# Top-k attention and a SwiGLU block on one core: weight rounding in pieces of 512 columns, the first K and Q split over two queues by head, and the first rounding step moved behind the start of the first top-k

## The chip, the core and the metric

The kernel runs on one core of one Trainium2 chip. The metric is the device time in microseconds (us) of one execution, lower being better; where several runs are taken, their median counts. Five units work side by side, each on its own list of instructions in order: TensorE (PE, matrix products; PEld is its weight load), VectorE (DVE), ScalarE (ACT), GpSimd (POOL) and the queues that issue DMA transfers (SP, and a few on ACT).[...]

## The reference

Attention keeps, for each query, the 32 largest of its 576 scores; the result goes through a gated feed-forward block (FFN). All is in 32-bit floats.

```python
# q, k, v: (8, 8, 576, 64)          top_k = 32
scores = scale * np.matmul(q, k.transpose(0, 1, 3, 2))
kth    = np.partition(scores, -top_k, axis=-1)[..., -top_k:-top_k + 1]
scores = np.where(scores >= kth, scores, -1000000000.0)
attn   = softmax(scores)                        # over the last axis
x      = (attn @ v).transpose(0, 2, 1, 3).reshape(4608, 512)
g      = x @ w_gate                             # (4608, 1536)
out    = (g * sigmoid(g) * (x @ w_val)) @ w_out # (4608, 512)
```

The weights arrive as 64-bit floats. The kernel reads them as pairs of 32-bit integers and makes 32-bit floats of them itself ("rounding" below).

## The kernel before

**Attention in units.** A unit is one batch, one tile of 128 queries and one pair of heads; there are 8 x 5 x 4 = 160 of them, and every fifth tile of a batch has only 64 queries, so that its two heads share the 128 partitions and the unit has half the work. For each unit PE makes the scores (L306 or L292), ACT copies them to SBUF (L311, L297), and DVE finds the 32 largest by four rounds of MAX8 (L327) with a MATCH_REPLACE8 (L331) between rounds, then writes a penalty for the values below the 32nd (L337). POOL adds the penalty to the scores (L349), ACT takes the exponential (L358) and scales it by the reciprocal of the sum (L370 on DVE, L373 on ACT), PE transposes the weights (`etps`, L385) and multiplies by V (L405, L414), and ACT copies the result into `xT` (L429).

**FFN in blocks.** The 4608 tokens form 18 blocks of 256. As soon as all four head pairs of a block are done, `feed` makes its products with `w_gate` and `w_val` (L468), the gate on ACT and POOL (L493 to L501), and the product with `w_out`. It gives these out in pieces of some 1.7 us of PE time. Block 0 uses a plain product (L514); the later ones use a scheme with seven instead of eight quarter products (L554), whose sums and differences of `w_out` POOL makes beforehand (L168 to L185).

**The order is written out by hand.** One loop over the units (L705 on) interleaves everything: unit n's top-k on DVE, the scores of unit n+1, the exponential of n-1, the transposes of n-3, the product with V of n-4, and FFN pieces paid from a credit (4.45 pieces for a full unit in the first 28 units, later a share that follows the unit's own PE work). At the end, a dependency without semaphore pins that order on PE, DVE, ACT and POOL. DMA issues on SP are not pinned.

**Weight rounding.** `rounded` handles one piece of 128 x 256 values in five stages: load 256 KB (L109); on ACT the absolute value of the high words and a scaling of the low words (L114, L116); on POOL a clamp (L119); on DVE a shift and mask (L123), followed on POOL by an integer addition (L126); on DVE a merge with sign and exponent into the destination `wg`, `wv` or `wo` (L129). There are 24 pieces for each of the three weights, 72 in all. `weights` is a generator; each of its steps moves several pieces by one stage, `lags` (L153) steps apart: at step n, piece n is loaded, piece n-2 has its ACT and clamp stages, piece n-3 its shift and addition, piece n-5 its merge. `early` (L158, called at L738) brings the ACT stage of the newest pieces forward at the start of a unit. Six buffers of each kind are in turn (`bufs=6`). A step is taken by `rounding(1)`, called in `dve` (L713 to L720): every VALUES step of the top-k adds 5/11 to `due`, and one step of rounding is due at each whole number, except in the first four steps of a unit (`beside=False`). Two steps are taken before the loads of the second pair of heads (L693), two more between the first unit's scores and the loop (L697). `need` makes more steps where an FFN product asks for a piece that isn't there yet; it takes the number of pieces.

**The first loads.** `load(i)` brings K and Q of a pair of heads: for each of K and Q one DMA per head, then one for the last 64 positions of both heads. For the first pair, K goes over SP and Q over ACT's queue (L217); all other loads go over SP.

Of the kernel before, what the change touches and what calls it, by code (L numbers as in the profile page):

```python
# [10 lines left out]
FP32 = mybir.dt.float32  # L11
I32 = mybir.dt.int32
# [3 lines left out]
P = 128  # L16
# [5 lines left out]
WP = 256  # L22
# [5 lines left out]
def kernel(  # L28
# [37 lines left out]
    nc = tc.nc  # L66
    B, H, S, D = q.shape
    DM, DFF = w_gate.shape
# [4 lines left out]
    KC = DM // P  # L73
    MC = DFF // P
    MS = MC // 2
    MQ = MC // 2
# [9 lines left out]
    conv = ctx.enter_context(tc.tile_pool(name="conv", bufs=2))  # L86
    ffn = ctx.enter_context(tc.tile_pool(name="ffn", bufs=2))
# [13 lines left out]
    wg = consts.tile([P, KC, DFF], FP32, name="wg")  # L101
    wv = consts.tile([P, KC, DFF], FP32, name="wv")
    wo = consts.tile([P, MC, DM], FP32, name="wo")

    def rounded(src, dst):

        n = dst.shape[1]
        w = ffn.tile([P, n, 2], I32, tag="w", name="w", bufs=6)
        nc.sync.dma_start(w[:], src.bitcast(I32).rearrange("p (f t) -> p f t", t=2))  # L109
        yield  # L110
        low, high = w[:, :, 0], w[:, :, 1]

        size = conv.tile([P, n], FP32, tag="size", name="size", bufs=6)
        nc.scalar.activation(size[:], high.bitcast(FP32), AF.Abs)  # L114

        nc.scalar.mul(low, low.bitcast(U32), 2.0**-29)  # L116
        yield

        nc.gpsimd.tensor_scalar(size[:], size[:], HUGE, LEAST, ALU.min, ALU.max)  # L119
        yield  # L120

        bits = size[:].bitcast(I32)
        nc.vector.tensor_scalar(  # L123
            bits, bits, 3, 0x3FFFFFFF, ALU.logical_shift_left, ALU.bitwise_and
        )
        nc.gpsimd.tensor_tensor(bits, bits, low, ALU.add)  # L126
        yield

        nc.vector.scalar_tensor_tensor(  # L129
            out=dst.bitcast(I32), in0=high, scalar=-0x40000000, in1=bits,  # L130
            op0=ALU.bitwise_and, op1=ALU.bitwise_or,
        )

    def weights():

        pieces = []
        for f in range(0, DFF, WP):
            for src, dst in ((w_gate, wg), (w_val, wv)):
                for c in range(KC):
                    pieces.append((src[c * P : (c + 1) * P, f : f + WP], dst[:, c, f : f + WP]))  # L140
        for c in range(MC):
            for f in range(0, DM, WP):
                pieces.append((w_out[c * P : (c + 1) * P, f : f + WP], wo[:, c, f : f + WP]))
        pieces = [rounded(*p) for p in pieces]
        step = [0] * len(pieces)

        def upto(i, k):

            while 0 <= i < len(pieces) and step[i] < k:
                next(pieces[i], None)  # L150
                step[i] += 1

        lags = (5, 3, 2, 2, 0)  # L153
        for n in range(len(pieces) + lags[0]):
            for k, lag in enumerate(lags):
                upto(n - lag, len(lags) - k)
            ready[0] = max(n - lags[0] + 1, 0)
            early[0] = lambda: [upto(n - 1, 2), upto(n, 2)]  # L158
            yield
        early[0] = lambda: None  # L160


        add, sub = ALU.add, ALU.subtract
        lo, hi = slice(0, DM // 2), slice(DM // 2, DM)
        for m in range(0, MQ, 2):
            mm, nn = slice(m, m + 2), slice(MQ + m, MQ + m + 2)
            t3 = ffn.tile([P, 2, DM // 2], FP32, tag="w", name="t3", bufs=6)
            nc.gpsimd.tensor_tensor(t3[:], wo[:, nn, hi], wo[:, mm, hi], sub)  # L168
            T[7] += [t3[:, i, :] for i in range(2)]
            yield  # L170
        while not plain_done:
            yield
        for m in range(0, MQ, 2):
            mm, nn = slice(m, m + 2), slice(MQ + m, MQ + m + 2)
            t1 = wo[:, mm, hi]
            nc.gpsimd.tensor_tensor(t1, t1, wo[:, mm, lo], sub)
            T[5] += [wo[:, m + i, hi] for i in range(2)]
            yield
            t2 = ffn.tile([P, 2, DM // 2], FP32, tag="w", name="t2", bufs=6)
            nc.gpsimd.tensor_tensor(t2[:], wo[:, nn, hi], t1, sub)  # L180
            T[6] += [t2[:, i, :] for i in range(2)]
            yield
            for i in range(2):
                t4 = conv.tile([P, DM // 2], FP32, tag="size", name="t4", bufs=6)
                nc.gpsimd.tensor_tensor(t4[:], wo[:, MQ + m + i, lo], t2[:, i, :], sub)  # L185
                T[4].append(t4[:])
            yield
        T[1] += [wo[:, m, lo] for m in range(MQ)]
        T[2] += [wo[:, MQ + m, lo] for m in range(MQ)]
        T[3] += [wo[:, MQ + m, hi] for m in range(MQ)]  # L190
        yield

    ready = [0]
    early = [lambda: None]
    plain_done = []
    T = {i: [] for i in range(1, 8)}
    weight = weights()

    def rounding(n):
        for _ in range(n):  # L200
            next(weight, None)

    def need(n):

        while ready[0] < n:
            next(weight)
# [4 lines left out]
    def load(i):  # L211
        b, hp = pairs[i]
        h = slice(2 * hp, 2 * hp + 2)
        kq = ld.tile([P, 2, J, 2, D], FP32, tag="kq", name="kq_in")
        kq_last = ld.tile([P, 2, D], FP32, tag="kql", name="kq_last")
        for n, src in ((0, k), (1, q)):
            queue = nc.scalar if n == 1 and i == 0 else nc.sync  # L217
            for hh in range(2):
                queue.dma_start(
                    kq[:, n, :, hh, :],  # L220
                    src[b, 2 * hp + hh, 0:JP].rearrange("(p j) d -> p j d", j=J),
                )
            queue.dma_start(
                kq_last[n * R : (n + 1) * R], src[b, h, JP:S].rearrange("h p d -> p h d")
            )
        raw[i] = (kq, kq_last)
# [209 lines left out]
    def store(o, g0):  # L436

        at = g0
        while at < g0 + P:
            b, c = divmod(at, S)  # L440
            j, p0 = divmod(c, P)
            n = min(g0 + P - at, S - c, P - p0)
            r0 = b * S + (c if j == J else J * p0 + j)
            dst = out[r0 : r0 + n, :] if j == J else out[r0 : r0 + J * (n - 1) + 1 : J, :]
            nc.sync.dma_start(dst, o[at - g0 : at - g0 + n, :])
            at += n
# [3 lines left out]
    def flush(queue):  # L450
        while queue:
            queue.pop(0)()

    def feed(kb):
# [6 lines left out]

        def product(w, s, then):
            ps = ps_f.tile([P, 2, BLK], FP32, tag="f", name="f")
            need(8 * s + (4 if w is wg else 8))
            for i in range(2):
                m = 2 * s + i
                for kc in range(KC):
                    nc.tensor.matmul(  # L468
                        ps[:, i, :],
                        w[:, kc, m * P : (m + 1) * P],  # L470
                        x[:, kc, :],
                        start=(kc == 0),
                        stop=(kc == KC - 1),
                    )
                if i == 1:
                    on_act.append(lambda: then(ps))
                yield 1
# [28 lines left out]
        if plain:  # L506
            for t in range(2):
                ps = ps_f.tile([P, DM], FP32, tag="f", name="o_ps")
                for m in range(MC):
                    need(8 * MS + 2 * m + 2)  # L510
                    if m == 6:
                        flush(on_act)
                        flush(on_pool)
                    nc.tensor.matmul(  # L514
                        ps[:],
                        hs[m // 2][:, m % 2, t * P : (t + 1) * P],
                        wo[:, m, :],
                        start=(m == 0),
                        stop=(m == MC - 1),
                    )  # L520
                    if m == MC - 1:

                        def finish(ps=ps, t=t):
                            nc.scalar.copy(o[:, t, :], ps[:])
                            store(o[:, t, :], kb * BLK + t * P)

                        on_act.append(finish)
                        if t == 1:
                            plain_done.append(True)
                    if m % 2 == 1:  # L530
                        yield 1
            return
# [149 lines left out]
    def run(steps):  # L682
        for _ in steps:
            pass
# [7 lines left out]
    load(0)  # L692
    rounding(2)  # L693
    load(1)
    run(fetch(0))
    run(scores(0))
    rounding(2)  # L697
    run(fetch(1))
    credit = [0.0]
    no = iter(())  # L700
    over = {}
    TURN, VALUES = 3, 4
    HEAD = 28
    due = [0.0]
    for n in range(NU + VALUES):  # L705
        nh = n_heads(units[n][1]) if n < NU else 1
        topk = select(n) if n < NU else no
# [106 lines left out]
```

## Time and profile before

Median of three runs: 1845.41 us (1844.97 to 1846.03). The profiled execution has a span of 1843.6 us.

| engine | busy us | share of span |
|---|---|---|
| PE | 1708.1 | 93% |
| DVE | 1623.5 | 88% |
| ACT | 1208.6 | 66% |
| POOL | 1026.2 | 56% |

| the rounding's instructions, 128x256 | engine | count | busy us | mean ns |
|---|---|---|---|---|
| L114 absolute value | ACT | 72 | 31.9 | 443 |
| L116 scaling | ACT | 72 | 31.6 | 439 |
| L119 clamp | POOL | 72 | 32.0 | 444 |
| L123 shift and mask | DVE | 72 | 21.3 | 296 |
| L126 addition | POOL | 72 | 54.4 | 755 |
| L129 merge into `wg`, `wv` | DVE | 48 | 19.4 | 404 |
| L129 merge into `wo` | DVE | 24 | 15.2 | 631 |

Shares of busy time are averages over stages that differ: in the first stage there are no FFN blocks to feed, and PE has little to do; in the last, DVE has finished. Mean durations on DVE include the overlap of an instruction's start with the end of the one before it, so the distance from start to start is what an instruction costs. The weights are rounded in the first 236 us. FFN work starts at 158 us.

### The profile page before, as it was taken

What the parts mean: (1) busy time and instruction counts of PE and PEld (TensorE: products, weight loads), DVE (VectorE), ACT (ScalarE), POOL (GpSimd) and SP (SyncE); (2) the same over time, 40 slices, a digit from 0 to 9 for tenths busy, and PEclk for the clock granted to TensorE, in tenths of its full rate; (3) what the DMA queues carried; (4) which work ended last, traced back from release to release, by engine and by line L of the source; (5) the groups of instructions that cost most, each with busy time, mean ns of one, the idle gap of its engine ahead of it and who ended that gap; (6) DMA issues with size and microseconds to landing.
All of it is one profiled execution on the core that took longest, in us unless ns stands there. A gap on an engine that the chain in (4) does not pass through costs nothing.

```text
span 1843.6 us, 30858 instructions
## 1 busy us (share of the span) xinstructions
PE 1708.1 (93%) x10756; PEld 1409.2 (76%) x10756; DVE 1623.5 (88%) x3477; ACT 1208.6 (66%) x3015; POOL 1026.2 (56%) x1007
## 2 busy tenths in 40 slices
PE   3447899999999989999999999999999999999998
PEld 2336658777788878887888878888788878888887
DVE  7999999999999979997999989998999989998400
ACT  5667757667666667676767675767676776675432
POOL 4666756645455644656464736564556554646444
PEclk7668999989999999999999999999999999999999
DMA  7332221000300021000300012000300011000000
GB/s 191 92 86 81 69 53 40 12 1 8 86 1 13 1 59 34 13 1 14 73 19 1 13 36 57 2 12 2 73 19 12 1 36 32 1 12 12 1 12 12
DMA packets 111260, 59.67 MB, mean 32 GB/s; under 512 B 89088, under 2 KB 97280, under 8 KB 111104
## 3 DMA queue, kind: packets, MB, share of 16 engines
q1 hardware_dynamic: 109904, 57.41, 11.8%
q8 instruction: 85, 1.39, 0.3%
q14 instruction: 71, 0.58, 0.1%
q10 hardware_dynamic: 1200, 0.30, 0.1%
HBM read 48.23 MB, written 9.44 MB: 31 GB/s over the span
## 4 chain that ended last, share of the span: by engine, by line
PE 83%; DVE 6%; ACT 3%; POOL 3%; issue 2%; DMA 0%; POOLq 0%; ACTq 0%
PE f L468 39%; PE x_ps L554 9%; PE av L414 8%; PE etps L385 7%; PE s L306 7%; PE y_ps L554 6%; DVE m L327 2%; DVE rest L331 2%; PE s L292 2%; PE av L405 1%; PE o_ps L514 1%; PE kqps L261 1%; POOL e L349 1%; ACT e L358 1%; DVE e L337 1%
## 5 line engine op out<-in xcount | busy, mean ns | idle before, releaser
L327 DVE MAX8 m<-rest 128x8 f32<-128x576 f32 x864 | 614.5, 745 | 2.2
L331 DVE MATCH_REPLACE8 rest<-m,rest 128x576 f32<-128x576 f32 x576 | 423.4, 741 | 0.0
L349 POOL TENSOR_TENSOR e<-e,sc 128x1152 f32<-128x1152 f32 (+1 forms) x160 | 382.7, 2392 | 67.2 <-DVE e L337 61.7
L468 PE MATMUL f<-xT,wg 128*128 128x256 f32 x1728 | 401.7, 382 | 0.0
L468 PE MATMUL f<-xT,wv 128*128 128x256 f32 x1728 | 398.9, 381 | 0.0
L468 PEld LDWEIGHTS f<-xT,wg 128*128 128x128 f32 x1728 | 322.8, 190 | 62.5 <-issue 20.5
L468 PEld LDWEIGHTS f<-xT,wv 128*128 128x128 f32 x1728 | 324.5, 190 | 58.5 <-issue 16.3
L496 POOL TENSOR_TENSOR h<-h,half_g 128x512 f32<-128x512 f32 x108 | 138.2, 1279 | 295.2 <-ACT h L495 289.6
L327 DVE MAX8 m<-sc 128x8 f32<-128x576 f32 x288 | 205.1, 748 | 99.1 <-ACT sc L297 58.3
L385 PE MATMUL etps<-ident,e 128*128 128x128 f32 (+1 forms) x1312 | 186.7, 287 | 104.3 <-POOL size L126 36.2
L358 ACT ACTIVATE e<-e,bias 128x576 f32<-128x576 f32 x288 | 222.1, 777 | 93.3 <-POOL e L349 93.2
L386 ACT COPY et<-etps 128x512 f32<-128x512 f32 (+1 forms) x448 | 184.3, 483 | 124.3 <-PE etps L385 122.9
L385 PEld LDWEIGHTS etps<-ident,e 128*128 128x128 f32 (+1 forms) x1312 | 159.6, 147 | 133.1 <-POOL size L126 39.0
L501 POOL TENSOR_TENSOR h<-h,val 128x512 f32<-128x512 f32 x108 | 140.2, 1298 | 193.2 <-ACT val L500 193.1
L373 ACT ACTIVATE e<-e,tot 128x576 f32<-128x576 f32 x288 | 211.9, 789 | 6.3 <-DVE tot L370 6.3
L331 DVE MATCH_REPLACE8 rest<-m,sc 128x576 f32<-128x576 f32 x288 | 211.6, 740 | 0.0
L306 PE MATMUL s<-kqT 64*128 64x288 f32 x1024 | 171.1, 447 | 4.4 <-ACT kqT L266 3.8
L414 PE MATMUL av<-et,v 128*64 128x128 f32 (+1 forms) x2560 | 173.8, 281 | 0.0
L337 DVE TENSOR_SCALAR e<-sc,m 128x576 f32<-128x576 f32 x288 | 165.4, 610 | 3.4
L311 ACT COPY sc<-s 128x288 f32<-128x288 f32 x512 | 163.9, 402 | 1.9 <-PE s L306 1.9
L414 PEld LDWEIGHTS av<-et,v 128*64 128x64 f32 x2560 | 136.8, 144 | 23.0 <-issue 7.1
L493 ACT ACTIVATE h<-f 128x512 f32<-128x512 f32 x108 | 65.4, 605 | 132.6 <-PE f L468 132.6
(71 smaller groups left out, 2042.1 us busy)
## 6 DMA issues: line engine op xcount, KB each, us to landing
kq_in<-in_k_dram SPq DMA_DIRECT2D x64, 128.0 KB, 2.8
v<-in_v_dram SPq DMA_DIRECT2D x32, 256.0 KB, 2.9
kq_in<-in_q_dram SPq DMA_DIRECT2D x62, 128.0 KB, 2.9
w<-in_moe_w_gate_dram SPq DMA_DIRECT2D x24, 256.0 KB, 2.7
w<-in_moe_w_val_dram SPq DMA_DIRECT2D x24, 256.0 KB, 2.7
w<-in_moe_w_out_dram SPq DMA_DIRECT2D x24, 256.0 KB, 2.5
out_dram<-o SPq DMA_DIRECT2D x40, 128.0 KB, 2.4
out_dram<-o SPq DMA_DIRECT2D x16, 256.0 KB, 2.4
```

The source lines that it names most:

```text
L306: nc.tensor.matmul(ps[:, 0:half], slab[d, q0 : q0 + P], slab[d, k0 : k0 + half])
L327: nc.vector.max(m[:, t, 8 * r : 8 * r + 8], cur[:, hs])
L331: nc.vector.match_replace(rest[:, hs], m[:, t, 8 * r : 8 * r + 8], cur[:, hs], LOWEST)
L337: nc.vector.tensor_scalar(e[:, hs], sc[:, hs], m[:, t, TOP_K - 1 : TOP_K], FAR, ALU.is_lt, ALU.mult)
L349: nc.gpsimd.tensor_tensor(e[:, every], e[:, every], sc[:, every], ALU.add)
L358: nc.scalar.activation(e[:, hs], e[:, hs], AF.Exp, bias=bias[:, t : t + 1], scale=scale, accum_out=tot[:, t : t + 1],)
L373: nc.scalar.mul(e[:, hs], e[:, hs], tot[:, t : t + 1])
L385: nc.tensor.transpose(ps[0:kl, c * P : (c + 1) * P], e[:, k0 : k0 + kl], ident[:])
L386: nc.scalar.copy(et[0:kl, c0 : c0 + cn, :], ps[0:kl, 0 : cn * P].rearrange("p (c j) -> p c j", c=cn),)
L414: nc.tensor.matmul(av[hh * R : (hh + 1) * R, 0:ql], v_last[:, hh, :] if c == J else vt[:, hh, c, :], moving, start=last and c == 0, stop=c ...
L468: nc.tensor.matmul(ps[:, i, :], w[:, kc, m * P : (m + 1) * P], x[:, kc, :], start=(kc == 0), stop=(kc == KC - 1),)
L554: nc.tensor.matmul(ps, lhsT, T[i][m], start=m == 0, stop=m == MQ - 1)
```

## The change

It does three things.

1. A piece is now 128 x 512 values: two row blocks of `w_gate` or `w_val`, or a whole row block of `w_out`. There are 36 pieces instead of 72, with three buffers of twice the size. A step of the generator now moves a piece only where `n - lag` is even, so that a piece takes the same number of steps as two pieces did. `need` counts in the new pieces. The temporary tiles of POOL's sums and differences of `w_out` are cut from three tiles allocated at once, and the last difference of each group is one instruction of 512 columns instead of two of 256.
2. Of the first pair's K and Q, head 0 goes over SP and head 1 over ACT's queue; the small loads of the last positions all go over SP.
3. The two steps of rounding ahead of the loop go away; `due` starts at 2 instead, so that they are taken behind the first two MAX8 of the first unit.

Its purpose is to spend fewer instructions, each with its fixed cost, on the rounding, and to let the first top-k start earlier.

```diff
     def rounded(src, dst):
-        n = dst.shape[1]
-        w = ffn.tile([P, n, 2], I32, tag="w", name="w", bufs=6)
-        nc.sync.dma_start(w[:], src.bitcast(I32).rearrange("p (f t) -> p f t", t=2))
+        w = ffn.tile([P, 2, WP, 2], I32, tag="w", name="w", bufs=3)
+        nc.sync.dma_start(w[:].rearrange("p c f t -> p c (f t)"), src.bitcast(I32))
         yield
-        low, high = w[:, :, 0], w[:, :, 1]
-        size = conv.tile([P, n], FP32, tag="size", name="size", bufs=6)
+        low, high = w[:, :, :, 0], w[:, :, :, 1]
+        size = conv.tile([P, 2, WP], FP32, tag="size", name="size", bufs=3)
...
         lags = (5, 3, 2, 2, 0)
-        for n in range(len(pieces) + lags[0]):
+        for n in range(2 * len(pieces) - 1 + lags[0]):
             for k, lag in enumerate(lags):
-                upto(n - lag, len(lags) - k)
-            ready[0] = max(n - lags[0] + 1, 0)
-            early[0] = lambda: [upto(n - 1, 2), upto(n, 2)]
+                if (n - lag) % 2 == 0:
+                    upto((n - lag) // 2, len(lags) - k)
+            ready[0] = max((n - lags[0]) // 2 + 1, 0)
+            early[0] = lambda: upto(n // 2, 2)
             yield
...
-            for i in range(2):
-                t4 = conv.tile([P, DM // 2], FP32, tag="size", name="t4", bufs=6)
-                nc.gpsimd.tensor_tensor(t4[:], wo[:, MQ + m + i, lo], t2[:, i, :], sub)
+            t4 = conv.tile([P, 2, DM // 2], FP32, tag="size", name="t4", bufs=3)
+            nc.gpsimd.tensor_tensor(t4[:], wo[:, nn, lo], t2, sub)
...
         for n, src in ((0, k), (1, q)):
-            queue = nc.scalar if n == 1 and i == 0 else nc.sync
             for hh in range(2):
+                queue = nc.scalar if hh == 1 and i == 0 else nc.sync
                 queue.dma_start(kq[:, n, :, hh, :], ...)
-            queue.dma_start(kq_last[n * R : (n + 1) * R], ...)
+            nc.sync.dma_start(kq_last[n * R : (n + 1) * R], ...)
...
     run(scores(0))
-    rounding(2)
     run(fetch(1))
...
-    due = [0.0]
+    due = [2.0]
```

More of the change, by code (lines that the diff above doesn't have):

```diff
@@ L105, in rounded @@
     def rounded(src, dst):
-        n = dst.shape[1]
-        w = ffn.tile([P, n, 2], I32, tag="w", name="w", bufs=6)
-        nc.sync.dma_start(w[:], src.bitcast(I32).rearrange("p (f t) -> p f t", t=2))
+        w = ffn.tile([P, 2, WP, 2], I32, tag="w", name="w", bufs=3)
+        nc.sync.dma_start(
+            w[:].rearrange("p c f t -> p c (f t)"), src.bitcast(I32)
+        )
         yield
-        low, high = w[:, :, 0], w[:, :, 1]
-        size = conv.tile([P, n], FP32, tag="size", name="size", bufs=6)
+        low, high = w[:, :, :, 0], w[:, :, :, 1]
+        size = conv.tile([P, 2, WP], FP32, tag="size", name="size", bufs=3)
         nc.scalar.activation(size[:], high.bitcast(FP32), AF.Abs)
@@ L138, in weights @@
             for src, dst in ((w_gate, wg), (w_val, wv)):
-                for c in range(KC):
-                    pieces.append((src[c * P : (c + 1) * P, f : f + WP], dst[:, c, f : f + WP]))
+                for c in range(0, KC, 2):
+                    rows = src[c * P : (c + 2) * P, f : f + WP]
+                    pieces.append((
+                        rows.rearrange("(c p) f -> p c f", p=P), dst[:, c : c + 2, f : f + WP]
+                    ))
         for c in range(MC):
-            for f in range(0, DM, WP):
-                pieces.append((w_out[c * P : (c + 1) * P, f : f + WP], wo[:, c, f : f + WP]))
+            pieces.append((
+                w_out[c * P : (c + 1) * P].rearrange("p (c f) -> p c f", c=2),
+                wo[:, c].rearrange("p (c f) -> p c f", c=2),
+            ))
         pieces = [rounded(*p) for p in pieces]
@@ L164, in weights @@
         lo, hi = slice(0, DM // 2), slice(DM // 2, DM)
+        room = []
+        for _ in range(3):
+            t = ffn.tile([P, 4, DM // 2], FP32, tag="w", name="t", bufs=3)
+            room += [t[:, 0:2], t[:, 2:4]]
         for m in range(0, MQ, 2):
             mm, nn = slice(m, m + 2), slice(MQ + m, MQ + m + 2)
-            t3 = ffn.tile([P, 2, DM // 2], FP32, tag="w", name="t3", bufs=6)
-            nc.gpsimd.tensor_tensor(t3[:], wo[:, nn, hi], wo[:, mm, hi], sub)
+            t3 = room.pop()
+            nc.gpsimd.tensor_tensor(t3, wo[:, nn, hi], wo[:, mm, hi], sub)
             T[7] += [t3[:, i, :] for i in range(2)]
@@ L178, in weights @@
             yield
-            t2 = ffn.tile([P, 2, DM // 2], FP32, tag="w", name="t2", bufs=6)
-            nc.gpsimd.tensor_tensor(t2[:], wo[:, nn, hi], t1, sub)
+            t2 = room.pop()
+            nc.gpsimd.tensor_tensor(t2, wo[:, nn, hi], t1, sub)
             T[6] += [t2[:, i, :] for i in range(2)]
             yield
-            for i in range(2):
-                t4 = conv.tile([P, DM // 2], FP32, tag="size", name="t4", bufs=6)
-                nc.gpsimd.tensor_tensor(t4[:], wo[:, MQ + m + i, lo], t2[:, i, :], sub)
-                T[4].append(t4[:])
+            t4 = conv.tile([P, 2, DM // 2], FP32, tag="size", name="t4", bufs=3)
+            nc.gpsimd.tensor_tensor(t4[:], wo[:, nn, lo], t2, sub)
+            T[4] += [t4[:, i, :] for i in range(2)]
             yield
@@ L222, in load @@
                 )
-            queue.dma_start(
+            nc.sync.dma_start(
                 kq_last[n * R : (n + 1) * R], src[b, h, JP:S].rearrange("h p d -> p h d")
@@ L463, in product @@
             ps = ps_f.tile([P, 2, BLK], FP32, tag="f", name="f")
-            need(8 * s + (4 if w is wg else 8))
+            need(4 * s + (2 if w is wg else 4))
             for i in range(2):
@@ L509, in feed @@
                 for m in range(MC):
-                    need(8 * MS + 2 * m + 2)
+                    need(4 * MS + m + 1)
                     if m == 6:
```

## The prediction

> **What bounds the kernel now.** I read first the table of busy time by stage, with stages cut where PE's waits change. Columns: busy us (and count) of PE, PEld, DVE, ACT, POOL, then granted PE clock, DMA share, GB/s.
>
> ```profile
> 0.00:46.00 46.00, 15.14 (x68) 9.89 (x68) 33.96 (x84) 25.07 (x70) 19.57 (x33) 0.72 0.73 192
> 46.00:138.00 92.00, 40.29 (x227) 31.85 (x227) 91.70 (x221) 61.17 (x166) 57.07 (x76) 0.63 0.31 88
> 138.00:249.00 111.00, 89.98 (x500) 68.35 (x500) 108.40 (x240) 77.39 (x196) 77.67 (x93) 0.92 0.20 65
> 249.00:361.00 112.00, 110.11 (x712) 87.17 (x709) 107.23 (x230) 76.63 (x196) 65.64 (x61) 1.00 0.15 37
> 361.00:383.00 22.00, 16.56 (x103) 13.34 (x105) 22.00 (x51) 14.36 (x39) 8.52 (x7) 0.69 0.07 25
> 383.00:1720.00 1337.00, 1320.47 (x8516) 1098.83 (x8516) 1246.95 (x2630) 913.27 (x2267) 740.80 (x677) 1.00 0.09 22
> ```
>
> PE is the bound from 249 us to 361 and from 383 to the end. Before 249 us it idles 103.6 us (249 less 15.1, 40.3 and 90.0), while DVE, once started at 12.6 us, hardly stops: 91.7 of 92 us, then 108.4 of 111. So the time is PE's fixed list of work plus the idle time that the DVE-bound opening leaves it. All rounding lies there. PE's order of instructions is the same in the changed program, and so is the order of top-k, exponentials and copies; a microsecond that DVE gains before 236 us starts the later list a microsecond earlier, as long as PE still waits for it. PE's waits before its transposes at 153, 185, 200, 229, 240 and 249 us are 8.4, 1.6, 3.4, 3.0, 0.8 and 1.4 us.
>
> Then DVE's timeline (start, duration): one step of rounding amid the top-k, at 60 us.
>
> ```profile
> 60.41 0.41 DVE L129 SCALAR_TENSOR_TENSOR wv<-w,size 128x256 int32<-128x256 int32 x1
> 60.74 0.29 DVE L123 TENSOR_SCALAR size<-size 128x256 int32<-128x256 int32 x1
> 60.94 0.08 DVE L331 MATCH_VALUE_LOAD rest<-m,rest 128x8 f32 x1
> ```
>
> Read the starts: the merge costs 0.33 us, the shift 0.20.[...]
>
> Third, the same engine beside POOL at 176 us, when FFN work has begun:
>
> ```profile
> 176.62 2.62 POOL L349 TENSOR_TENSOR e<-e,sc 128x1152 f32<-128x1152 f32 x1
> 179.20 1.45 POOL L501 TENSOR_TENSOR h<-h,val 128x512 f32<-128x512 f32 x1
> ```
> ```profile
> 177.35 2.17 DVE L129 SCALAR_TENSOR_TENSOR wo<-w,size 128x256 int32<-128x256 int32 x1
> 179.45 1.36 DVE L123 TENSOR_SCALAR size<-size 128x256 int32<-128x256 int32 x1
> ```
>
> The merge takes 2.17 us and ends just after POOL's addition ends (179.24); the shift takes 1.36 and ends with the next POOL product (180.65). These are stalls, not work. For the 24 merges into `wo` they come to 15.2 - 24 x 0.405 = 5.5 us, for the long shift 1.1, and DVE waited twice 1.0 for POOL's clamp: **8.6 us** between 158 and 236 us. The merges into `wg` and `wv` (395 to 416 ns) never stall.
>
> [...] MAX8 ran beside POOL's additions at its usual length.[...] In this trace an issue takes 0.63 us, the landing about 3.
>
> **The change, part by part.**
>
> *Halved count on DVE.* Two merges and two shifts of 256 cost 1.06 us.[...] Saved: 0.13 x 36 = **4.7 us**, all on DVE's path before 236 us.[...]
>
> *Collisions with POOL.* Only twelve merges into `wo` now meet POOL, each twice as long. If a meeting costs what it did, half of 8.6 stays; POOL's own pieces get longer (below), so I leave 60%: **3.4 us** saved, with 0 and 8.6 as bounds.
>
> *The penalty (L337).* Pairs of it take 1.17 to 1.43 us beside POOL's rounding, and 0.92 at 232.8, with POOL idle. POOL's addition goes from 0.755 us to about 1.28 (L496, 128x512), and directly before L337 it can hold DVE 0.5 us longer. In half of some 17 units: 0 to 4.3 us lost. I take **1.2 lost**[...].
>
> *Start.* K's second DMA was issued behind the first, at about 1.5 us; now both go at 0.72. PE's first transpose, which waited for K until 5.94, moves up by about 0.8, and so do the first scores: head 0's were ready near 11.5, now 10.7. But this is what DVE met before:
>
> ```profile
> 11.67 0.44 ACT L114 ACTIVATE size<-w 128x256 f32<-128x256 f32 x1
> 12.64 0.29 DVE L123 TENSOR_SCALAR size<-size 128x256 int32<-128x256 int32 x1 [11.22 <-POOL size L119]
> 12.84 1.41 DVE L327 MAX8 m<-sc 128x8 f32<-128x576 f32 x2
> ```
>
> Now two MAX8 run first, until about 12.1, and the shift is third. It waits for the clamp, this for ACT's first rounding instruction, and that now stands behind the four copies of the second pair (ACT ends those near 13.0: with 0.63 us an issue, their last load goes out near 7.3, takes 3 to land, and transposes and copies follow). ACT 0.6 (L493's 605 ns for 512), clamp 0.65 (between 0.40 and 0.80), shift 0.33: the first REPLACE starts near 14.7, against 14.23. Of this 0.5, 0.13 is extra work done ahead. **0.4 lost**, from 1.0 lost to 1.3 won.
>
> *Added waits elsewhere.* A load is 512 KB. It may be issued at the merge one step ahead of it and is needed by the shift four steps later: 4 x 1.95 = 7.8 us (merges at 60.41 and 62.40). The chain is 2.7 landing (median for w) + 1.1 for another 256 KB at 240 GB/s + 0.6 ACT + 0.65 clamp = 5.1. Slack 2.7; cost nothing. Behind the waiting ACT instruction stand the exponentials and the copies of scores, which DVE needs, but these wait for L349 anyway (3.0 us idle at 69.4). Between a shift and the next, POOL needs 1.28 + 0.65 and DVE takes 3.9: free, where no FFN product stands between.
>
> *ACT and POOL.* ACT falls by 36 x 2 x (0.88 - 0.61) = 19 us, POOL by 36 x (2.40 - 1.93) = 17 and 0.4 for the merged differences. They aren't the bound, and that is worth nothing except in the collisions above.
>
> Sum: 4.7 + 3.4 - 1.2 - 0.4 = 6.5 us on DVE by 236 us. PE's waits after 184 us are 10.2, more than what is gained there, so PE follows to 249; the idle 5.4 of 361 to 383, DVE-paced as well, moves along. I count 0.9 for local mismatch: 5.9. 1845.4 - 5.9 = **1839.5**.
>
> **The rivals.**
>
> - *Few but long collisions*: the 8.6 stays.[...] 4.7 - 1.2 - 0.4 = 3.1, times 0.9: 1842.6.
> - *A new wait in the pipeline, slower*: with pieces twice as long and products of 1.28 or additions of 2.63 us in POOL's queue, the clamp is late. If 20 of 36 shifts wait 0.5 us, 10 lost against 3.1: 6.9 x 0.9: 1851.6. For it: the shift waited 1.0 for the clamp at 170 and 202 us. Against: POOL is idle 30 to 40% in these stages, and the distance between shifts doubles too.
> - *Better*: collisions vanish, the start wins 1.3, L337 loses nothing: (4.7 + 8.6 + 1.3) x 0.9 = 13.1: 1832.3.
>
> **The chances.** Forecast 0.55, few but long 0.22, slower 0.12, better 0.11. The bound of 0.2% is 3.7 us: faster means under 1841.7. Of the forecast's spread most lies below that, of the second case little: faster 0.65, same 0.22, slower 0.13. The range 1834 to 1846 takes in the second case, no change, and part of the better one; it leaves out 0.12 and some 0.07.
>
> **What would show it.** Starts of merge and shift 0.60 and 0.33 apart before 150 us; last merge near 230 us instead of 235.95; merges into `wo` with 2 to 6 us of stalls in all; the first shift idle some 2 us behind two MAX8; PE's first FFN product near 155 us instead of 158.5. Wrong would be: shifts waiting for the clamp at many steps, ACT waiting for weights beyond 46 us, L337 pairs above 1.6 us, or PE without waits before 249 us.

## The result, and the profile after

The changed kernel takes 1838.26 us (median of six runs, 1837.33 to 1839.80) against 1845.82 us of the kernel before on the same chip: ratio 0.9959, 95% interval 0.9946 to 0.9972. On another occasion it was 1839.18 against 1843.72, ratio 0.9975 (0.9966 to 0.9984). By these medians it is 4.5 to 7.6 us faster; 5.9 were forecast.

The table of busy time by stage of the changed kernel, cut as before (busy us and count of PE, PEld, DVE, ACT, POOL, then granted PE clock, DMA share, GB/s):

```profile
46.00:138.00 92.00, 39.09 (x231) 31.34 (x232) 91.50 (x197) 60.47 (x138) 52.76 (x46) 0.65 0.32 94
138.00:249.00 111.00, 95.20 (x537) 70.92 (x536) 107.88 (x214) 77.56 (x175) 72.67 (x64) 0.94 0.20 62
249.00:361.00 112.00, 108.89 (x706) 87.39 (x704) 107.59 (x235) 77.59 (x198) 67.41 (x59) 0.98 0.15 40
383.00:1720.00 1337.00, 1320.46 (x8512) 1098.60 (x8511) 1244.51 (x2626) 914.29 (x2263) 741.26 (x677) 0.99 0.09 22
```

DVE is as full as before up to 249 us, with fewer instructions; PE does 5.2 us more work in the second row (95.20 against 89.98); the long stage behind is the same. PE's first FFN product starts at 155.83 us instead of 158.51. The last merge starts at 224.85 instead of 235.95, earlier than the 230 forecast: it comes one step of the generator sooner, and so already ahead of the 16th penalty instead of behind it.

One step of the rounding in DVE's timeline (start, duration):

```profile
59.54 0.69 DVE L130 SCALAR_TENSOR_TENSOR wv<-w,size 128x512 int32<-128x512 int32 x1
60.13 0.43 DVE L124 TENSOR_SCALAR size<-size 128x512 int32<-128x512 int32 x1
60.46 0.10 DVE L343 MATCH_VALUE_LOAD rest<-m,rest 128x8 f32 x1
```

From start to start the merge costs 0.59 and the shift 0.33. The forecast had 0.60 and 0.33, an estimate of mine that the trace of the kernel before, with no DVE instruction of 512 columns, did not show. 256 columns more cost 0.26 us in the merge (0.59 - 0.33) and 0.13 in the shift (0.33 - 0.20). By these starts I estimate the fixed cost at 0.07 us in either (0.33 - 0.26 and 0.20 - 0.13). The groups of merges (count, then busy us, mean ns, idle before):

```profile
L130 DVE SCALAR_TENSOR_TENSOR wo<-w,size 128x512 int32<-128x512 int32 x12 | 10.4, 866 | 0.1
L130 DVE SCALAR_TENSOR_TENSOR wg<-w,size 128x512 int32<-128x512 int32 x12 | 8.3, 688 | 0.0
```

The twelve merges into `wo` exceed the others by 10.4 - 8.3 = 2.1 us; two waits for the clamp in that stage add 0.74 and 0.51. The stalls beside FFN work fell from 8.6 us to 3.4.

Times of whole executions of one kernel scatter by 1 to 5 us, so I also use a finer measure: the start of the same penalty in two traces (L337 in the kernel before, L349 after, 160 of them, one or one pair for each unit). Up to the 21st, DVE's list shows how far a kernel is ahead; from the 21st to the 33rd the lead of each kernel stays within some 0.1 us. "Pairs" is the summed duration of the first 16 penalties; 16 x 0.93 = 14.9 would be without any hindrance. Every kernel named is told below.

| kernel | ratio to before (95%) | ahead at the 1st / 11th / 21st penalty, us | pairs, us |
|---|---|---|---|
| before | 1 | 0 | 20.0 |
| changed | 0.9959 (0.9946 to 0.9972) | -0.7 / 2.8 / 6.7 | 21.2 |
| changed, again | 0.9975 (0.9966 to 0.9984) | -0.5 / 1.5 / 5.5 | 23.1 |
| e1 pieces only | 0.9969 (0.9957 to 0.9980) | -0.5 / 2.6 / 6.6 | 22.2 |
| e2 start only | 1.0000 (0.9991 to 1.0008) | 0.0 / 0.1 / 0.1 | 20.2 |
| e3 later first step | 0.9961 (0.9949 to 0.9974) | 2.2 / 5.7 / 8.1 | 21.1 |
| e3 again | 0.9970 (0.9958 to 0.9982) | 2.3 / 4.3 / 7.0 | 24.0 |
| e4 gap before the penalty | 0.9944 (0.9931 to 0.9956) | 1.4 / 6.9 / 11.0 | 16.1 |
| e4 again | 0.9941 (0.9928 to 0.9954) | 1.9 / 7.4 / 11.5 | 15.9 |
| e5 before, no products | 0.9959 (0.9946 to 0.9971) | 0.3 / 0.3 / 7.9 | 20.0 |
| e6 changed, no products | 0.9955 (0.9942 to 0.9967) | -0.2 / 1.9 / 9.5 | 22.0 |
| e7 gap with 256 | 1.0018 (1.0009 to 1.0028) | 0.2 / -1.5 / -1.7 | 16.9 |
| e8 DVE in halves | 1.0006 (0.9998 to 1.0015) | -0.8 / -2.7 / -0.1 | 24.0 |

### The profile page after: what moved, and what is told of

It reads as the page before. It is cut to its first block, busy times and chain, and to the rows that moved or that the text cites. A ratio compares the mean times of both kernels' runs of the same rounds, so it can differ in the third digit from the quotient of the medians.

```text
span 1838.0 us, 30521 instructions
## 1 busy us (share of the span) xinstructions
PE 1708.0 (93%) x10756; PEld 1408.7 (77%) x10756; DVE 1616.3 (88%) x3405; ACT 1205.6 (66%) x2943; POOL 1014.3 (55%) x932
## 4 chain that ended last, share of the span: by engine, by line
PE 83%; ACT 2%; POOL 2%; DVE 1%; issue 1%; DMA 0%; POOLq 0%; ACTq 0%
PE f L480 39%; PE x_ps L566 9%; PE av L426 8%; PE etps L397 7%; PE s L318 7%; PE y_ps L566 6%; PE s L304 2%; PE av L417 1%; PE o_ps L526 1%; PE kqps L273 1%; DVE m L339 1%; POOL p L552 0%; ACT e L370 0%; DVE rest L343 0%; POOL h L614 0%
## 5 line engine op out<-in xcount | busy, mean ns | idle before, releaser
L339 DVE MAX8 m<-rest 128x8 f32<-128x576 f32 x864 | 621.6, 764 | 2.2
L343 DVE MATCH_REPLACE8 rest<-m,rest 128x576 f32<-128x576 f32 x576 | 428.7, 760 | 0.0
L349 DVE TENSOR_SCALAR e<-sc,m 128x576 f32<-128x576 f32 x288 | 170.2, 636 | 3.4
```

What stands on the lines that cost most here:

```text
L339: nc.vector.max(m[:, t, 8 * r : 8 * r + 8], cur[:, hs])
L343: nc.vector.match_replace(rest[:, hs], m[:, t, 8 * r : 8 * r + 8], cur[:, hs], LOWEST)
L349: nc.vector.tensor_scalar(e[:, hs], sc[:, hs], m[:, t, TOP_K - 1 : TOP_K], FAR, ALU.is_lt, ALU.mult)
```

## Experiments: which part of the change it is

**e1: the pieces alone.** The changed kernel with the old loads and the old two steps ahead of the loop.

```diff
-                queue = nc.scalar if hh == 1 and i == 0 else nc.sync
+                queue = nc.scalar if n == 1 and i == 0 else nc.sync
...
     run(scores(0))
+    rounding(2)
     run(fetch(1))
...
-    due = [2.0]
+    due = [0.0]
```

> Only the pieces of 512 columns; loads of the first pair and the two rounding steps ahead of the loop as in the kernel before. Theory A (the gain is DVE's: half the fixed costs of merges and shifts, fewer stalls behind POOL): nearly the whole gain stays, 1838 to 1839 us, ratio to before about 0.996, since the new start was worth nothing (the first REPLACE stood at 14.87 us after, 14.23 before). Theory B (the gain comes from the earlier start and loads): 1845, ratio 1.000.

Measured: 1838.84 us against 1844.58, and 6.6 us ahead at the 21st penalty, as the whole change (6.7). So the gain lies in the pieces, and theory B falls; that it is DVE's, as theory A says, the experiments of the next section show.

**e2: the start alone.** The kernel before with the new loads and the rounding steps moved; pieces of 256.

```diff
-            queue = nc.scalar if n == 1 and i == 0 else nc.sync
             for hh in range(2):
+                queue = nc.scalar if hh == 1 and i == 0 else nc.sync
...
-    rounding(2)
     run(fetch(1))
...
-    due = [0.0]
+    due = [2.0]
```

> Only the new loads of the first pair and the rounding steps moved behind the first two MAX8, with pieces of 256 columns. Theory A: the first MAX8 starts near 10.9 us instead of 12.84, but the shift behind it waits for ACT and POOL until about 14, so the first REPLACE stands where it did: 1845 to 1847 us, ratio 0.9995 to 1.0005. Theory B: 1838 to 1840.

Measured: 1844.40 us against 1844.58. DVE's timeline of e2 shows why nothing is won:

```profile
10.82 1.42 DVE L327 MAX8 m<-sc 128x8 f32<-128x576 f32 x2 [9.41 <-ACT sc L311]
13.94 0.29 DVE L123 TENSOR_SCALAR size<-size 128x256 int32<-128x256 int32 x1 [1.70 <-POOL size L119]
14.15 0.09 DVE L331 MATCH_VALUE_LOAD rest<-m,sc 128x8 f32 x1
14.22 0.74 DVE L331 MATCH_REPLACE8 rest<-m,sc 128x576 f32<-128x576 f32 x1
```

The first MAX8 starts 2.0 us earlier than before (12.84), and DVE then idles 1.70 us at the shift. The first REPLACE starts at 14.22; before it was 14.23. The bracket gives the idle time and what ended it.

In the changed kernel the same wait, with longer pieces. The timeline, with ACT and POOL:

```profile
10.89 1.42 DVE L339 MAX8 m<-sc 128x8 f32<-128x576 f32 x2 [9.48 <-ACT sc L323]
...
13.06 0.67 ACT L115 ACTIVATE size<-w 128x512 f32<-128x512 f32 x1
...
13.81 0.61 POOL L120 TENSOR_SCALAR size<-size 128x512 f32<-128x512 f32 x1 [12.52 <-ACT size L115]
...
14.46 0.43 DVE L124 TENSOR_SCALAR size<-size 128x512 int32<-128x512 int32 x1 [2.15 <-POOL size L120]
```

ACT comes to the rounding only after the copies of the second pair of heads, the clamp follows at 13.81, and the shift at 14.46.

**e3: the first step later still.** The changed kernel with one number changed, so that the first shift stands behind nine steps of the first top-k instead of two.

```diff
-    due = [2.0]
+    due = [0.0]
```

> The changed kernel with due starting at 0 instead of 2, so that the first shift stands behind nine steps of the first unit's top-k instead of two. Theory A: the 2.15 us that DVE idled at that shift go away and nothing else changes: 1836 us, ratio to before 0.9948. Rival: the rounding runs one piece later all along and meets POOL's FFN products once more often, or the shift pattern falls worse against the penalty; the 2 us are given back: 1838 to 1840.

Measured: 1836.76 us, ratio 0.9961. Its DVE timeline has no wait at the first shift, where the changed kernel had 2.15 us (the second shift, at 21.15, waits 0.51):

```profile
10.63 1.42 DVE L339 MAX8 m<-sc 128x8 f32<-128x576 f32 x2 [9.22 <-ACT sc L323]
...
16.85 0.42 DVE L124 TENSOR_SCALAR size<-size 128x512 int32<-128x512 int32 x1
```

It leads the changed kernel by 2.8 us at the first and the 11th penalty, but only by 1.4 at the 21st. Between the 15th and the 17th it gives back 1.7: the rounding runs later, so that three merges instead of two stand behind the 15th penalty, and with a shift that is 0.9 us of work that was only put off; and the 16th pair of penalties takes 1.87 us instead of 0.94. Run again beside the changed kernel:

> The changed kernel again, beside e3 and e4 on the same chip. 1837 to 1839 us, ratio to before 0.996.

> e3 again. By the traces 1.4 us ahead of the changed kernel at the 21st penalty (2.8 at the first, given back between the 15th and the 17th), so 1 to 2 us faster; the rival, all given back by the end: within 0.5 us.

Measured: 1837.82 us against 1839.18, and 7.0 against 5.5 us ahead. So 1.4 to 1.5 us stay of the 2.15, by the traces of both occasions; the times alone don't settle it, as the intervals overlap.

## Experiments: what in the pieces it is

**e8: DVE in halves.** The changed kernel, but DVE does each merge and each shift in two instructions of 256 columns. Loads, ACT and POOL stay at 512.

```diff
-        nc.vector.tensor_scalar(
-            bits, bits, 3, 0x3FFFFFFF, ...)
+        for c in range(2):
+            nc.vector.tensor_scalar(
+                bits[:, c], bits[:, c], 3, 0x3FFFFFFF, ...)
...
-        nc.vector.scalar_tensor_tensor(out=dst.bitcast(I32), in0=high, ...)
+        for c in range(2):
+            nc.vector.scalar_tensor_tensor(out=dst[:, c].bitcast(I32), in0=high[:, c], ...)
```

> The changed kernel, but with each merge and each shift on DVE done in two instructions of 256 columns; pieces stay at 512 for the loads, ACT and POOL. 72 more DVE instructions. Theory A (the fixed cost of DVE's instructions is 4.7 us of the gain): DVE reaches the 16th penalty some 4.7 us later than in the changed kernel, so about 2 us ahead of the kernel before; 1842 to 1843.5 us. Theory C (the gain comes from fewer instructions on ACT and POOL or fewer loads): it stays near 1838 us and near 6.7 us ahead.

Measured: 1845.12 us against 1844.26. The whole gain is gone, more than theory A had said; theory C falls, since the loads, ACT and POOL still work in 36 pieces here, and POOL's merged differences of `w_out` are kept too. The step at 60 us in DVE's timeline of e8:

```profile
60.56 0.73 DVE L133 SCALAR_TENSOR_TENSOR wv<-w,size 128x256 int32<-128x256 int32 x2
61.22 0.48 DVE L125 TENSOR_SCALAR size<-size 128x256 int32<-128x256 int32 x2
61.62 0.07 DVE L346 MATCH_VALUE_LOAD rest<-m,rest 128x8 f32 x1
```

61.62 - 60.56 = 1.06 us for what took 60.46 - 59.54 = 0.92 in one piece: 36 x 0.14 = 5.0 us, the term forecast as 4.7. Summed from start to start over all merges and shifts the difference is 4.7 us too (each instruction's start to the next start, less idle time between). The rest of the loss of 6.7 up to the 21st penalty is the penalties, 2.9 us more (the pairs alone 24.0 instead of 21.2), less 0.9 us by which DVE idles less. Against the second trace of the changed kernel, whose pairs take 23.1, the loss is 5.6, with 4.9 from merges and shifts and 0.9 from the penalties.

**e5 and e6: POOL's products left out in block 0.** In both kernels POOL doesn't multiply the gate in block 0, so that POOL is free beside the rounding of `w_out`. Block 0's output lacks the gate; the same edit in both:

```diff
-                on_pool.append(lambda: nc.gpsimd.tensor_mul(h[:], h[:], half[:]))
+                if not plain:
+                    on_pool.append(lambda: nc.gpsimd.tensor_mul(h[:], h[:], half[:]))
...
-                on_pool.append(lambda: nc.gpsimd.tensor_mul(h[:], h[:], val[:]))
+                if not plain:
+                    on_pool.append(lambda: nc.gpsimd.tensor_mul(h[:], h[:], val[:]))
```

> The kernel before without POOL's products in block 0 (the gate isn't applied there, 12 products of 1.28 us left out), so that POOL is free beside the rounding of w_out. Theory A (8.6 us of stalls of merges, shifts and clamps there are POOL's products and the additions they push back): most of it goes, DVE's 16th penalty comes 6 to 9 us earlier, 1837 to 1840 us. Theory D (these long merges have another cause): within 2 us of the kernel before.

> The changed kernel with the same products left out. Theory A: its smaller stalls (3.6 us) and part of the penalty's excess (4.2 us in units 10 to 15) go, 4 to 6 us; so the two kernels without products differ by 3 to 5 us at the 16th penalty instead of 6.7. Theory D: they differ by 6.7 as before.

Measured: 1835.26 and 1835.36 us against 1844.26. The groups of merges into `wo`, of e5 and of e6:

```profile
L129 DVE SCALAR_TENSOR_TENSOR wo<-w,size 128x256 int32<-128x256 int32 x24 | 10.2, 423 | 0.0
```
```profile
L130 DVE SCALAR_TENSOR_TENSOR wo<-w,size 128x512 int32<-128x512 int32 x12 | 8.1, 677 | 0.0
```

Without the products the means fall from 631 to 423 ns and from 866 to 677, near the 404 and 688 of the merges into `wg`: the stalls are all but gone, so the products, with the additions that they push back, caused them. The time of e5 is below the 1837 to 1840 expected. The kernel before gains 7.9 us at the 21st penalty from this alone (its stalls were 8.6), the changed one 2.8 (9.5 - 6.7) or, against its second trace, 4.0. So the change had cut the loss beside the products by 3.9 to 5.1 us. My number for the distance between e5 and e6 missed: 1.5 us at the 21st penalty, not 3 to 5. I had left out what the longer pieces cost. Up to the 21st penalty merges and shifts cost 5.0 us less in e6 than in e5 from start to start, but the penalties 2.7 more (their pairs take 22.0 against 20.0), and DVE idles 0.7 longer, start and waits for the clamp together.

**e4: a gap before the penalty.** In the changed kernel a pair of penalties takes up to 2.61 us. One such place in its timelines, with a pair of 2.00, DVE first, then POOL:

```profile
154.96 0.43 DVE L124 TENSOR_SCALAR size<-size 128x512 int32<-128x512 int32 x1
155.29 2.00 DVE L349 TENSOR_SCALAR e<-sc,m 128x576 f32<-128x576 f32 x2
```
```profile
155.53 1.44 POOL L127 TENSOR_TENSOR size<-size,w 128x512 int32<-128x512 int32 x1 [1.84 <-ACT xT L441]
```

The addition starts during the first penalty and ends near 156.97 (155.53 + 1.44); the pair ends at 157.29 (155.29 + 2.00) and takes 2.00 us instead of 0.93. e4 keeps the rounding away from the last two MAX8 of a unit, so that the addition can end first; the steps move to the other eight positions at a higher rate (each top-k step behind the first four of a unit adds to `due`: ten in a full unit, eight here). It includes e3's edit.

```diff
-                due[0] += 5 / 11 if beside else 0
+                due[0] += 25 / 44 if beside else 0
...
-        dve(2)
+        dve(1)
+        dve(1, beside=False)
         run(topk)
```

> As e3, and no rounding step beside the last two MAX8 of a unit (rate 25/44 on the eight steps left instead of 5/11 on ten). POOL's addition of 1.29 us then has two MAX8 (1.33 us) to finish before the penalty, which in the changed kernel took 6.2 us more than 0.93 for a pair in the first 16 units. Theory A: most of that goes, 1832 to 1834 us, ratio 0.993. Rival: the steps stand closer (every 1.76 instead of 2.2 steps of top-k), shifts wait for the clamp, and the time is 1838 or more.

Measured: 1833.77 us against 1844.58. The pairs fall to 16.1 us. The same unit in e4, POOL then DVE:

```profile
150.15 1.29 POOL L127 TENSOR_TENSOR size<-size,w 128x512 int32<-128x512 int32 x1 [1.17 <-issue]
```
```profile
151.24 0.95 DVE L349 TENSOR_SCALAR e<-sc,m 128x576 f32<-128x576 f32 x2
```

The addition is nearly through when the pair begins. It runs 2.9 us ahead of e3 at the 21st penalty, less than the 5.0 us by which the pairs shrank: its merges into `wo` take 12.0 us in all against 10.4, and its shifts wait 4.2 us for the clamp against 2.7. So the rival is true in part. Again, beside the changed kernel:

> e4 again. By the traces its 21st penalty stands 4.3 us ahead of the changed kernel's, so 4 us faster than that one in the same call, ratio to before 0.994; if the difference of e4 was chance between calls, within 1 us of it.

Measured: 1832.79 us against 1839.18; the intervals of the two ratios, 0.9928 to 0.9954 and 0.9966 to 0.9984, lie apart. This is the fastest of the kernels that compute the whole reference.

**e7: the same gap with pieces of 256.** The kernel before with the edit of e4.

> The kernel before (pieces of 256, old start), with no rounding step beside the last two MAX8 of a unit, as in e4. Theory A: the pairs of penalties fall from 19.9 us in the first 16 units towards 15, 3 to 4 us gained, 1841 us. Rival: POOL has only 0.3 us to spare between shift and shift with pieces of 256, and with steps every 1.76 instead of 2.2 steps of top-k the shifts wait for the clamp; no gain, 1845 or more.

Measured: 1847.00 us against 1844.26, ratio 1.0018, so a little slower. The pairs fell to 16.9 us, as theory A said, but DVE's waits in the first 250 us are now

```profile
DVE size L123 <- POOL size L119: 15.4, 16, 11.0
```

that is 16 waits of 15.4 us in all; the longest, 11.0, is the start, so the others come to 4.4 us, against 2.3 (13.5 - 11.2) in the kernel before. All merges are held longer, those into `wg` and `wv` too, which were not held before (404 ns):

```profile
L129 DVE SCALAR_TENSOR_TENSOR wo<-w,size 128x256 int32<-128x256 int32 x24 | 16.1, 669 | 0.0
L129 DVE SCALAR_TENSOR_TENSOR wv<-w,size 128x256 int32<-128x256 int32 x24 | 10.4, 432 | 0.0
L129 DVE SCALAR_TENSOR_TENSOR wg<-w,size 128x256 int32<-128x256 int32 x24 | 10.2, 427 | 0.0
```

From start to start up to the 21st penalty, the penalties win 3.2 us, the merges lose 2.9 and the waits 1.9, which is the 1.7 of the table within 0.1. The rival is right: with short pieces POOL did not finish between the closer steps (waits of 4.4 us against 2.3). Of the two lengths tried, the gap pays with the longer pieces only.

## Why the prediction was right

The 5.9 us forecast lie between the 4.5 and 7.6 measured. The stated range, 1834 to 1846 us, took in no change as well, so the time alone says little of the mechanism; the experiments and DVE's list do. "From start to start" below sums all of DVE's instructions up to the 21st penalty.

- **Halved count on DVE**, 4.7 us: shown. The step of 0.92 us fits the 0.60 + 0.33 forecast; e8 puts the term at 4.7 to 5.0, from start to start it is 4.4, with every merge taken at the mean of those into `wg` and `wv` and the long shift left out.
- **Collisions with POOL**, 3.4 us saved: the mechanism is shown by e5 and e6, the size was too low. Of 8.6 us 3.4 to 3.6 stayed, not 5.2, so some 5.1 were saved; by e5 and e6 the saving is 3.9 to 5.1.
- **The penalty**, 1.2 us lost: shown in kind by e4, too small in size. From start to start it is 1.5 in one trace and 3.5 in the other (in the pairs alone 21.2 - 20.0 = 1.2, and 3.1). The second trace is behind the first by 1.2 us at the 21st penalty, and the first step of that is one pair, the fourth, with 1.98 us in place of 0.96. In the first trace it was POOL's addition beside this pair that took longer, 1.87 us (L127 at 64.41) where the one before it took 1.30. So about a microsecond looks to hang on which of the two engines is held; POOL's side of the second trace was not shown.
- **Start**, 0.4 us lost: about right. DVE is 0.7 us behind at the first penalty, by which it has done more of the rounding. Two MAX8, an idle shift of 2.15 us (some 2 were forecast) and the first REPLACE at 14.87 (14.7 forecast) came as worked out. e2 shows that the part is worth nothing.
- **Waits elsewhere at nothing**: not quite. Besides the start and the two in the `w_out` stage, shifts waited 1.0 us for the clamp (4.4 in all, less 2.15, 0.74 and 0.51), against 0.3 before. These are two waits of 0.51 us, shown below. The 240 GB/s in the forecast's chain is near what the kernel before moved from 24 to 26 us (241) and from 26 to 28 (273).
- **PE follows**: shown. PE still waited after 184 us, and the lead at the 21st penalty, 6.7 and 5.5 us in the two traces of the changed kernel, is 5.8 and 6.1 at the last. The factor of 0.9 set 0.6 us aside for mismatch. Traces can't tell so small an amount: e2, level with the kernel before at the 33rd penalty (0.1 us), is 2.4 ahead at the 38th, because DVE waits for scores 0.7 us there instead of 3.1. The granted PE clock in 361 to 383 us had been 0.84 in e2 against 0.69; whether this is the cause wasn't tested. The changed kernel gains nothing at that place.

Of the two waits of 0.51 us elsewhere, at 127 and 139 us, this is the second, DVE first, then POOL:

```profile
138.34 0.69 DVE L130 SCALAR_TENSOR_TENSOR wg<-w,size 128x512 int32<-128x512 int32 x1
139.54 0.43 DVE L124 TENSOR_SCALAR size<-size 128x512 int32<-128x512 int32 x1 [0.51 <-POOL size L120]
```
```profile
138.60 0.91 POOL L120 TENSOR_SCALAR size<-size 128x512 f32<-128x512 f32 x1 [1.57 <-DVE rest L343]
```

The clamp starts beside the merge and takes 0.91 us instead of 0.61 (1.14 at 127 us). So it looks held by DVE's own merge, and the shift behind the merge then waits for it; the forecast counted only FFN products as what could come between. No run takes the merge away, so this cause is read from the trace and not tested.

In the first trace the terms nearly close on the lead: 4.4 + 5.1 - 1.5 - 0.6 (start) - 0.9 (waits elsewhere, with 0.1 before a merge) = 6.5 of 6.7; most of the rest is in the value loads, 0.2. That they come to the 6.5 forecast is partly luck: the collisions gave 1.7 us more, and every other term came out 0.2 to 0.9 worse. In the second trace the penalties take 2.0 us more than in the first, and the lead is 5.5.

Two of the four signs of being wrong did appear. Pairs of penalties took more than 1.6 us, up to 2.61: that is the penalty term above. And ACT waited for weights beyond 46 us, 9.0 us in nine waits up to 250 us (2.1 in three before); none of them led to one of DVE's waits for the clamp. Of the rivals, "few but long collisions" fell with the group of merges into `wo`; the slower one, late clamps, appeared only at some steps here, and in full in e7.

## What to carry to other kernels

Where one engine sets the pace, as DVE did here up to 249 us, count its small instructions: halving them was worth their fixed cost times the number saved, 36 x 0.14 = 5.0 us by e8, and nothing else of the change had to be faster. From that goes what the longer instructions hold up elsewhere, here 1.5 to 3.5 us at the penalties. Where one engine's instructions grow longer beside another's, look first at what is queued directly behind the instruction that hands over to the other engine: here a pair of penalties stood there and took 2.00 us instead of 0.93 beside an addition of 1.44. Moving the hand-over ahead of two MAX8 was worth 2.9 to 4.5 us at the 21st penalty (e4 against e3), about half of the whole change or more; with short pieces it cost time (e7). An instruction moved behind the start of a critical list gained nothing in e2 (ratio 1.0000), where what feeds it did not move with it: the list started 2.0 us earlier and then idled 1.70 us for POOL's clamp.

## What the runs showed of the hardware

A merge, a shift and a pair of penalties on DVE took longer beside a POOL instruction: 2.17 us instead of 0.41, 1.36 instead of 0.29, 2.00 instead of 0.93. They ended 0.28, 0.16 and 0.32 us behind the end of that instruction. This time is recorded inside the instruction: none of the three shows idle time before it. In the pair of 2.00 us the first penalty took 0.53 and the second 1.57, beside the addition that ran from 155.53 to 156.97. Beside POOL's addition to the scores (L349 of the kernel before, 2.62 and 2.64 us) MAX8 kept 0.67 us from start to start (at 176.68) and MATCH_REPLACE8 0.66 (at 160.85). The 152 MAX8 up to the 21st penalty take 102.3 to 102.6 us in every trace, 0.67 each, however long the penalties are.

I had not expected that two executions of one kernel would differ by 1 us or more in steps, through single pairs of penalties that take 0.96 us in one execution and 1.98 in the other. Nor that recorded durations on DVE grow along one trace without the work being slower: in the changed kernel a MATCH_REPLACE8 is recorded with 0.74 us near 15 us and 0.81 near 714, with 0.66 between starts (without its value load) in both places. Starts, not durations, were the measure to trust.
